# Two heads, or four batches, per chunk over the partitions, A before B, and one buffer ring, in a cached-attention decode kernel

## The chip, the cores and the metric

The kernel runs on one core of one Trainium2 chip. The metric is the device time of one execution in microseconds (us). The kernel before takes 1435.16 us, the median of three runs (1434.9 to 1435.97).

Engines are named as in the profile: PE (matmuls; PEld is its weight load), DVE (vector), ACT (scalar), POOL (GpSimd) and SP, which issues nearly all DMAs (295 of 297 in the DMA view of the kernel before).

## The reference

Two independent attention decode steps, each with one query token per batch and four batches. A has 32 query heads that share 8 key/value heads and looks at the last 2048 keys only. B has 32 heads with their own keys and values and looks at all 8192. The results are concatenated.

```python
def _A_ref(x, k_cache, v_cache, wq, wo):          # 4 batches, D = 512, Dh = 128
    W = min(4096, max(256, Sk // 4))              # 2048
    q = (x @ wq).reshape(B, Sq, Hq, Dh).transpose(0, 2, 1, 3)
    k = jnp.repeat(k_cache[:, :, Sk - W:, :], rep, axis=1)     # rep = 4
    v = jnp.repeat(v_cache[:, :, Sk - W:, :], rep, axis=1)
    p = softmax(einsum("bhqd,bhkd->bhqk", q, k) * Dh ** -0.5)
    o = einsum("bhqk,bhkd->bhqd", p, v)
    return o.transpose(0, 2, 1, 3).reshape(B, Sq, Hq * Dh) @ wo
# _B_ref: the same without window and repeat, 32 heads of 8192 keys
```

Everything is bf16. B's caches are 537 MB, A's windows 33.5 MB, the weights 17 MB. All of it is read once, so the kernel is a long stream of loads with some matmuls behind it.

## The kernel before

One chunk is 2 MB of K and 2 MB of V: one head of one batch (B), or one KV head of all four batches (A). For each 128 keys PE transposes K (T), multiplies it with the query (S), and later multiplies V with the probabilities (PV). B's 128 chunks come first, A's 8 last. K has a ring of 4 buffers and V one of 5.

A chunk always fills all 128 partitions with one DMA. In B a partition gets 64 consecutive keys, one contiguous run of 16 KB in HBM. In A it gets 16 consecutive keys of each batch, four runs of 4 KB:

```python
def kv_src(T, ch):
    if ch["ab"] == 1:
        return T[ch["b"], ch["h"]].rearrange("(p j) d -> p (j d)", p=P)
    return T[:, ch["g"], SkA - W:, :].rearrange("b (p j) d -> p b (j d)", p=P)

def dma_k(c):                                     # dma_v likewise, ring of NVB = 5
    ...
    waits = [("T", (c - NKB + 1) * NG - 1)] if c >= NKB else []
    sch.add_dma("sp", lambda e: e.dma_start(dst, src), ..., waits=waits, key=("k", c))
```

The scores of a chunk are 64 columns in B and 256 in A (64 tiles of 4 queries, each tile of one batch). The loads of the last three V come after all K:

```python
loads.insert(min(2 * c + 1, NC - 1 + c) if c < NC - 3 else len(loads), ("v", c))
```

## Time and profile before

| | value | where it is read |
|---|---|---|
| span | 1432.8 us | page |
| PE, DVE, ACT busy | 84%, 41%, 29% | page, part 1 |
| DMA share on the plateau | 0.99 to 1.01 at 415 to 426 GB/s | windows |
| chain that ended last | 79% DMA | page, part 4 |

The page's rows of the 40 equal slices, and the chain that ended last:

```profile
DMA  9999999999999999999999999999999999998995
GB/s 401 422 425 424 424 423 425 424 427 420 425 424 425 424 423 424 426 425 422 422 426 424 408 416 423 425 424 393 423 426 422 414 411 426 422 419 345 367 398 223
...
DMA 79%; PE 19%; DVE 1%; issue 0%; SPq 0%; ACT 0%; DVEq 0%
```

The DMA engines are busy for 80% or more of every slice but the last. The windows view of the same kernel (columns: the stretch in us, its length, busy us and number of instructions of each engine, granted PE clock, share of the DMA engines, GB/s):

```profile
40.00:80.00 40.00, 33.84 (x803) 32.41 (x800) 17.20 (x35) 12.76 (x22) 0.00 (x0) 1.00 1.01 426
800.00:1000.00 200.00, 168.96 (x3842) 159.39 (x3839) 82.39 (x173) 61.00 (x93) 0.00 (x0) 0.98 0.99 415
1280.00:1320.00 40.00, 33.85 (x784) 31.87 (x781) 16.74 (x36) 12.29 (x19) 0.00 (x0) 1.00 0.87 359
1360.00:1400.00 40.00, 32.04 (x659) 28.46 (x659) 18.40 (x51) 9.99 (x12) 0.00 (x0) 0.96 1.03 397
1420.00:1433.00 13.00, 9.54 (x172) 6.22 (x169) 1.21 (x4) 0.00 (x0) 0.00 (x0) 0.85 0.02 7
```

The first lines are B, the third is the turn to A, the fourth is A with its 4 KB runs, the last is the tail without loads.

The trace also has a record of every DMA packet. In the kernel before, the median packet takes 46 ns for 1 KB, 159 ns for 4 KB, 613 ns for 16 KB and 1213 ns for 32 KB (only the two query weights have runs of that length). So time per byte falls a little as runs grow: 46 ns a KB at 1 KB, 38.3 at 16 KB, 37.9 at 32 KB.

### The profile page before, as it was taken

To read this page: it belongs to the slowest core of one execution; us is meant where nothing else is said; L and a number is where in the kernel's file an instruction comes from. 1 tells how busy PE (TensorE), PEld (TensorE's weight loads), DVE (VectorE), ACT (ScalarE), POOL (GpSimd) and SP (SyncE) were. 2 spreads that over 40 slices of the span, in tenths; PEclk is the share of its full clock that TensorE was granted. 3 is DMA by queue.
4 is the path that set the end of the run, shared out by engine and by line. 5 is a ranking of instruction groups with operands and counts; after the bars stand their busy time and mean duration, and the time that the engine had idled before them with its cause. 6 is when DMAs were issued, how large, how long until landed. Compare 5 with 4: busy or idle time off the path is not lost.

```text
span 1432.8 us, 56273 instructions
## 1 busy us (share of the span) xinstructions
PE 1203.7 (84%) x26928; PEld 1133.7 (79%) x26928; DVE 590.2 (41%) x1267; ACT 421.8 (29%) x627; POOL 2.7 (0%) x11
## 2 busy tenths in 40 slices
PE   4888888888888888888898878888988898988787
PEld 4888887877778887888787878788878788887776
DVE  1434444444443443434344434444444343444444
ACT  0323322323222322323232323232322332333221
POOL 0000000000000000000000000000000000000000
PEclk8999999999999999999999999999999999999999
DMA  9999999999999999999999999999999999998995
GB/s 401 422 425 424 424 423 425 424 427 420 425 424 425 424 423 424 426 425 422 422 426 424 408 416 423 425 424 393 423 426 422 414 411 426 422 419 345 367 398 223
DMA packets 54356, 590.83 MB, mean 412 GB/s; under 512 B 4704, under 2 KB 12912, under 8 KB 21104
## 3 DMA queue, kind: packets, MB, share of 16 engines
q1 hardware_dynamic: 54112, 587.23, 97.9%
q8 instruction: 211, 3.46, 1.0%
q14 instruction: 17, 0.14, 0.0%
q10 hardware_dynamic: 16, 0.01, 0.0%
HBM read 587.21 MB, written 0.01 MB: 410 GB/s over the span
## 4 chain that ended last, share of the span: by engine, by line
DMA 79%; PE 19%; DVE 1%; issue 0%; SPq 0%; ACT 0%; DVEq 0%
DMA kn<-in_B_k_cache_dram 66%; PE tr L273 9%; DMA kn<-in_A_k_cache_dram 7%; DMA vn<-in_B_v_cache_dram 5%; PE po L385 4%; PE sc L302 4%; DMA vn<-in_A_wq_dram 2%; PE ms L334 1%; PE ms L320 0%; DVE kt L280 0%; PE fin L415 0%; PE ms L255 0%; PE ms L391 0%; DVE rm L314 0%; DVE tmp L353 0%
## 5 line engine op out<-in xcount | busy, mean ns | idle before, releaser
L273 PE MATMUL tr<-identb,kn 128*128 128x128 bf16 x8704 | 689.5, 224 | 186.4 <-DMA kn<-in_B_k_cache_dram 165.3
L280 DVE COPY kt<-tr 128x1024 bf16<-128x1024 bf16 x726 | 501.9, 691 | 700.9 <-PE tr L273 696.9
L273 PEld LDWEIGHTS tr<-identb,kn 128*128 128x128 bf16 x8704 | 520.6, 100 | 204.6 <-DMA kn<-in_B_k_cache_dram 180.0
L278 ACT ACTIVATE kt<-tr 128x1024 bf16<-128x1024 bf16 x362 | 370.4, 1023 | 856.7 <-PE tr L273 850.9
L385 PE MATMUL po<-pb,vn 128*128 128x64 bf16 x8704 | 450.6, 195 | 10.4 <-issue 9.3
L302 PE MATMUL sc<-qs,kt 128*128 128x64 bf16 x8704 | 453.3, 195 | 4.5 <-issue 3.6
L302 PEld LDWEIGHTS sc<-qs,kt 128*128 128x128 bf16 x8704 | 377.8, 100 | 10.3 <-issue 4.8
L385 PEld LDWEIGHTS po<-pb,vn 128*128 128x128 bf16 x8704 | 344.1, 99 | 23.9 <-issue 22.7
L342 ACT ACTIVATE pb<-sc,negb 128x64 bf16<-128x64 f32 x128 | 39.9, 312 | 122.5 <-DVE negb L336 122.5
L334 PE MATMUL ms<-gm,nsc 1*128 1x1 f32 x256 | 48.5, 256 | 0.5 <-issue 0.4
L334 PEld LDWEIGHTS ms<-gm,nsc 1*128 1x128 f32 x256 | 37.5, 182 | 14.1 <-issue 0.5
L322 DVE TENSOR_REDUCE gm<-ms 1x1 f32<-1x128 f32 (+1 forms) x136 | 37.0, 272 | 20.6 <-PE ms L320 20.6
L314 DVE TENSOR_REDUCE rm<-sc 128x1 f32<-128x64 f32 (+1 forms) x136 | 31.3, 230 | 29.1 <-PE sc L302 29.1
L320 PE MATMUL ms<-identf,rm 128*1 128x128 f32 (+1 forms) x136 | 38.4, 282 | 1.6 <-DVE rm L314 1.6
L336 DVE COPY negb<-ms 128x1 f32<-128x1 f32 (+1 forms) x136 | 20.8, 153 | 30.0 <-PE ms L334 30.0
L342 ACT ACTIVATION_READ_ACCUMULATOR pb<-sc,negb 128x1 f32 x128 | 25.1, 196 | 0.0
L415 PE MATMUL fin<-wor,oT 128*4 128x512 bf16 x64 | 21.1, 393 | 2.7 <-DVE oT L398 2.7
L320 PEld LDWEIGHTS ms<-identf,rm 128*1 128x1 f32 (+1 forms) x136 | 11.6, 85 | 13.5 <-DVE rm L314 13.4
L255 PE MATMUL ms<-xT,vn 128*128 128x4 bf16 x256 | 7.1, 166 | 10.4 <-DMA vn<-in_A_wq_dram 6.0
L398 DVE TENSOR_TENSOR oT<-po,rinv 128x4 bf16<-128x4 f32 (+1 forms) x40 | 6.3, 158 | 21.9 <-PE po L385 21.9
L255 PEld LDWEIGHTS ms<-xT,vn 128*128 128x128 bf16 x256 | 7.0, 104 | 10.6 <-DMA vn<-in_A_wq_dram 6.1
L391 PE MATMUL ms<-rs,onesf 128*128 128x4 f32 (+1 forms) x80 | 13.8, 244 | 1.1 <-DVE rs L360 1.1
(26 smaller groups left out, 51.7 us busy)
## 6 DMA issues: line engine op xcount, KB each, us to landing
kn<-in_B_k_cache_dram SPq DMA_DIRECT2D x128, 2048.0 KB, 32.4
vn<-in_B_v_cache_dram SPq DMA_DIRECT2D x128, 2048.0 KB, 36.9
kn<-in_A_k_cache_dram SPq DMA_DIRECT2D x8, 2048.0 KB, 20.7
vn<-in_A_v_cache_dram SPq DMA_DIRECT2D x7, 2048.0 KB, 21.9
vn<-in_B_wq_dram SPq DMA_DIRECT2D x1, 4096.0 KB, 12.2
vn<-in_A_wq_dram SPq DMA_DIRECT2D x1, 4096.0 KB, 27.3
wor<-in_B_wo_dram SPq DMA_DIRECT2D x8, 512.0 KB, 37.9
wor<-in_A_wo_dram SPq DMA_DIRECT2D x8, 512.0 KB, 18.3
```

Source lines behind the costliest of these rows:

```text
L273: sch.add("pe", lambda e, o=o, i_=i_: e.transpose(o, i_, identb[:, :]), waits=waits, key=("T", s) if t == TG - 1 else None)
L278: sch.add("act", lambda e: e.activation(dst, src, ACTF.Copy), waits=waits, key=("ev", s))
L280: sch.add("dve", lambda e: e.tensor_copy(dst, src), waits=waits, key=("ev", s))
L302: sch.add("pe", lambda e, o=o, l=l, q=q: e.matmul(o, l, q, start=True, stop=True), waits=waits, key=("S", s) if t == TG - 1 else None)
L314: sch.add("dve", lambda e: e.tensor_reduce(out=dst, in_=src, axis=AX.X, op=ALU.max), waits=[("S", (c + 1) * NG - 1)], key=("rowmax", c))
L320: sch.add("pe", lambda e: e.transpose(ms[0:n, col:col + P], rm[:, m, 0:n], identf[:, :]), waits=[("rowmax", c), "c_identf"] + ms_read, key ...
L322: sch.add("dve", lambda e: e.tensor_reduce(out=gm[0:n, m, :], in_=ms[0:n, col:col + P], axis=AX.X, op=ALU.max), waits=[("trm", c)], key=(" ...
L334: sch.add("pe", lambda e: e.matmul(ms[:, col:col + n], nsc[0:n, :], rhs, start=True, stop=True), waits=[("dg", c) if n > 1 else ("gmax", c ...
L336: sch.add("dve", lambda e: e.tensor_copy(negb[:, m, 0:n], ms[:, col:col + n]), waits=[("bc", c)], key=("negb", c))
L342: sch.add("act", lambda e: e.activation(pbv, sc[:, c % 2, 0:NT], ACTF.Exp, bias=negb[:, m, 0:1], scale=scale, accum_out=ri), waits=[("negb ...
L385: sch.add("pe", lambda e, o=o, l=l, r=r, jj=jj: e.matmul(o, l, r, start=(jj == 0), stop=(jj == J - 1)), waits=waits, key=("pv", c) if j == ...
L415: sch.add("pe", lambda e, o=o, l=l, r=r, st=st, sp_=sp_: e.matmul(o, l, r, start=st, stop=sp_), waits=[("oT", c), ("wo", ch["wo_i"])] if i ...
```

## The change

The intent is longer HBM runs. A B chunk becomes two heads of one batch: head 0 on partitions 0 to 63, head 1 on 64 to 127, 128 keys per partition, runs of 32 KB, 4 MB per load. An A chunk becomes four batches on 32 partitions each, 64 keys per partition, runs of 16 KB. As the partitions of a tile now belong to different heads or batches, the probability matrix has a column for each (2 in B, 16 in A) and zeros in the other blocks, so that one matmul still serves the tile. A goes first, so that its small chunks are not at the end. K and V share one ring of ten 2 MB halves, and the last V comes in four pieces.

```diff
+        chunks.append(dict(ab=0, U=NB, C=REP, g=g, wo=g, NT=NB * W // P, norm=g, last=True, n0=0))
+            chunks.append(dict(ab=1, U=2, C=1, hp=hp, b=b, wo=Hkv + hp // 2, NT=2 * SkB // P, ...))
-        kn = sb("kn", [P, NKB, NT * P], BF16)
-        vn = sb("vn", [P, NVB, NT * P], BF16)
+        kv = sb("kv", [P, NH, 8192], BF16)                       # NH = 10
...
+            if ch["ab"] == 0:
+                PP = P // NB
+                for b in range(NB):
+                    src = T[b, ch["g"], SkA - W:, :].rearrange("(pp j) d -> pp (j d)", pp=PP)
+                    sch.add_dma("sp", lambda e, b=b, src=src: e.dma_start(kv[b * PP:(b + 1) * PP, at, :], src),
+                                "d_h%d" % at, waits=waits, key=(kind, c) if b == NB - 1 else None)
                 return
+            src = T[ch["b"], 2 * ch["hp"]:2 * ch["hp"] + 2].rearrange("u (pp j) d -> (u pp) (j d)", pp=P // 2)
...
+            for u, pp in blocks(c):        # A: each block of partitions keeps its own 4 of 16 columns
+                src = sc[pp, half, :].rearrange("p (j x) -> p j x", x=16)[:, :, u * REP:(u + 1) * REP]
+                sch.add("dve", lambda e, src=src, dst=dst: e.tensor_copy(dst, src), ...)
...
-            loads.insert(min(2 * c + 1, NC - 1 + c) if c < NC - 3 else len(loads), ("v", c))
+            loads.insert(2 * c + 1 if c < NC - 3 else len(loads), ("v", c))
```

Cut: the row maximum, exponential and sum on blocks of partitions, PV waits by ring slot, and the schedule.

## The prediction

> **What bounds the kernel now.** The DMA engines. In the windows view their busy share is 0.99 to 1.01 from 40 to 1280 us, at 415 to 426 GB/s; PE is busy 84% of the span, DVE 41%, ACT 29%. The chain of waits is 79% DMA, nearly all K loads. So bytes, time per packet and the ends of the program matter. The DMA packet records give that time: median 46 ns for 1 KB, 159 ns for 4 KB (A's K and V), 613 ns for 16 KB (B's), 1213 ns for 32 KB (the two wq loads): about 13 ns plus 600 ns for each 16 KB.
>
> A's 8192 packets of 4 KB run at 371 to 397 GB/s (windows 1320 to 1400). At the turn from B to A (1280 to 1320) the rate falls to 359 GB/s, about 6 us lost. After the last loads (about 1417 us) PE still multiplies late V chunks; the span ends at 1432.8, about 16 us in which the DMA does almost nothing.
>
> **What the change does.** Bytes and PE work (8704 transposes, score and PV matmuls each) stay. Costs on DMA:
> - B: 16384 packets of 32 KB: 16384 x 1213 / 16 = 1242 us for 1255; gain 13 us.
> - A: 4 KB becomes 16 KB; gain 4 us by the medians, and about 6 us of the dip at the turn.
> - Tail: the last V comes in pieces, the last of 16 tiles; the PV of the two chunks before is done by then. After the last landing: 16 matmuls, scaling, two output matmuls, a copy, the store: about 6 us for 16; gain 10 us.
> - Ring of ten halves: I estimate over 14 us of queued loads at the tightest moment, so no new waits. Statistics on half or quarter partitions add DVE and ACT operations of 0.2 to 0.4 us; both have room.
>
> The sum is -33 us: about 1401 us, if A's loads run at full rate.
>
> **The doubt.** A's chunk is now loaded by four DMAs of 32 partitions. [...] No DMA of before has this shape, so its trace can't say. [...] I give this 55%.
>
> **Prediction.** 1440 us, eight in ten between 1396 and 1480. Faster by over 2%: 0.38; within 2%: 0.35; slower by over 2%: 0.27. All of it is critical, as DMA is the bound throughout.
>
> **What would show it.** B's packets: 1213 ns, about 428 GB/s on the plateau. [...] Tail: under 7 us from the last V landing to the end. Chain of waits: still K loads, no ring wait that empties the DMA.
>
> **What would make it wrong.** [...] PE stalls in A's longer statistics chain that delay slot release; 4 MB granularity emptying the queue; a slow engine among 16 that sets each landing.

Without the doubt the sum came to -33 us, about 1401 us. The doubt, that A's new loads run slower, put 40 to 78 us on it (1440 to 1480 us) at 55%. These 40 to 78 us rested on no trace. The 0.2 to 0.4 us of a statistics operation are what the trace of the kernel before has (means of 0.15 to 0.42 us). For the 6 us of the tail the same trace has 1.99 us for 64 PV matmuls, 1.04 us for four output matmuls and 0.68 us for the last copy.

## The result, and the profile after

The change takes 1507.2 us (1506.58 to 1508.09, 4 runs) against 1435.03 us: ratio 1.0503, 95% interval [1.0485, 1.0521]. It is 5% slower, outside the stated range.

The page of the kernel after, its slices and chain:

```profile
DMA  9999999999999999999999999999999999999995
GB/s 313 211 215 218 217 339 427 429 429 426 426 428 429 427 424 429 427 427 424 417 421 413 426 426 412 428 412 424 425 418 418 423 425 422 419 419 425 423 424 223
...
DMA 56%; PE 33%; issue 4%; DVE 4%; SPq 2%; another core or an unknown queue 0%; ACT 0%; DVEq 0%
```

And its windows view:

```profile
80.00:120.00 40.00, 22.10 (x346) 19.88 (x344) 17.04 (x40) 5.75 (x8) 0.00 (x0) 0.76 1.01 214
240.00:280.00 40.00, 34.02 (x831) 32.40 (x826) 17.65 (x33) 13.85 (x20) 0.00 (x0) 1.00 1.01 429
800.00:1000.00 200.00, 166.03 (x3825) 158.16 (x3823) 83.20 (x160) 63.06 (x93) 0.00 (x0) 0.96 1.00 420
1480.00:1490.00 10.00, 9.31 (x236) 8.87 (x233) 5.57 (x10) 3.37 (x4) 0.00 (x0) 1.00 0.49 205
1490.00:1500.00 10.00, 9.16 (x290) 8.89 (x291) 0.75 (x4) 0.91 (x4) 0.00 (x0) 1.00 0.28 113
```

The loss has a place. While A is loaded, up to about 210 us, the DMA engines count as fully busy (1.01) and move 214 GB/s. They are not waiting: each packet takes twice as long. In the packet records of 80 to 120 us the median 16 KB packet takes about 1235 ns, where the kernel before needs 613 ns for that size, and the 1 KB packets of the output weights in between take about 90 ns, not 46. A DMA share of 1 does not say that the loads run at full rate; the GB/s beside it does. PE, at 55% in this stretch, is not the limit.

Priced from these records: 2048 packets of 16 KB times (1230 - 613) ns over 16 engines is 79 us, and 4096 packets of 1 KB times 45 ns over 16 is 12 us.

B then runs at 425 to 429 GB/s, against 424 before, but only up to about 600 us; from 600 to 800 us it is 424, later 420 to 422. And in the tail the DMA engines don't finish together: the share is 0.49 at 1480 to 1490 us and 0.28 at 1490 to 1500. The landings shown further down fit this: eight of 16 come near 1480 us, the other eight near 1496.

### The profile page after: what moved, and what is told of

Its sections match the earlier page's. It is cut to its first block, busy times and chain, and to the rows that moved or that the text cites. A ratio compares the mean times of both kernels' runs of the same rounds, so it can differ in the third digit from the quotient of the medians.

```text
span 1504.7 us, 55575 instructions
## 1 busy us (share of the span) xinstructions
PE 1184.0 (79%) x26704; PEld 1124.8 (75%) x26704; DVE 622.7 (41%) x1211; ACT 443.5 (29%) x651; POOL 4.5 (0%) x12
## 3 DMA queue, kind: packets, MB, share of 16 engines
q8 instruction: 208, 3.41, 0.9%
## 4 chain that ended last, share of the span: by engine, by line
DMA 56%; PE 33%; issue 4%; DVE 4%; SPq 2%; another core or an unknown queue 0%; ACT 0%; DVEq 0%
DMA kv<-in_B_k_cache_dram 48%; PE tr L310 15%; PE po L437 8%; PE sc L340 8%; DMA kv<-in_A_k_cache_dram 8%; SPq L225 2%; DVE kt L317 2%; PE ms L392 1%; DVE rm L369 1%; PE ms L376 1%; PE fin L473 0%; DVE rsa L419 0%; ACT pba L417 0%; DVE sA L354 0%
## 5 line engine op out<-in xcount | busy, mean ns | idle before, releaser
L310 PE MATMUL tr<-identb,kv 128*128 128x128 bf16 x8704 | 708.5, 227 | 172.0 <-DMA kv<-in_B_k_cache_dram 83.2
L310 PEld LDWEIGHTS tr<-identb,kv 128*128 128x128 bf16 x8704 | 535.3, 102 | 185.1 <-DMA kv<-in_B_k_cache_dram 89.1
L437 PE MATMUL po<-pbb,kv 128*128 128x64 bf16 x8192 | 419.1, 194 | 50.9 <-issue 50.7
L437 PEld LDWEIGHTS po<-pbb,kv 128*128 128x128 bf16 x8192 | 319.6, 99 | 63.6 <-issue 63.0
L405 ACT ACTIVATE pbb<-sc,negb 64x128 bf16<-64x128 f32 x128 | 51.5, 402 | 81.8 <-DVE negb L394 80.5
L369 DVE TENSOR_REDUCE rm<-sc 64x1 f32<-64x128 f32 x128 | 36.5, 286 | 17.6 <-PE sc L340 16.7
L437 PE MATMUL po<-pba,kv 128*128 128x64 bf16 x512 | 32.8, 219 | 1.5 <-issue 1.1
L392 PE MATMUL ms<-identf,gx 1*128 1x1 f32 (+1 forms) x144 | 28.4, 264 | 2.4 <-DVE gx L384 1.8
L437 PEld LDWEIGHTS po<-pba,kv 128*128 128x128 bf16 x512 | 25.7, 115 | 5.2 <-issue 4.7
L405 ACT ACTIVATION_READ_ACCUMULATOR pbb<-sc,negb 64x1 f32 x128 | 23.7, 185 | 0.0
```

The source lines that it names most:

```text
L310: sch.add("pe", lambda e, o=o, i_=i_: e.transpose(o, i_, identb[:, :]), waits=waits, key=("T", s) if t == TG - 1 else None)
L369: sch.add("dve", lambda e, src=src, pp=pp: e.tensor_reduce(out=rm[pp, m, 0:1], in_=src, axis=AX.X, op=ALU.max), waits=[("S", ch["s_last"]) ...
L392: sch.add("pe", lambda e: e.matmul(ms[:, col:col + C], gx[0:C, m, :], identf[0:C, 0:C], start=True, stop=True), waits=[("gx", c)] + ms_rea ...
L405: sch.add("act", lambda e, src=src, pp=pp, ri=ri, u=u: e.activation(pbv[pp, :, u], src, ACTF.Exp, bias=negb[pp, m, 0:1], scale=scale, accu ...
L437: sch.add("pe", lambda e, o=o, l=l, r=r, j=j: e.matmul(o, l, r, start=(j == 0), stop=(j == ch["NT"] - 1)), waits=waits, key=("pv", c) if j ...
```

## The experiments

The main theory: that each of A's DMAs covers only 32 neighbouring partitions is what halves its rate, and this alone costs the time. Rivals: the small size and larger number of A's DMAs; going first; A's longer statistics chain; the one ring. Runs marked wrong load other data; their amount of work is that of the change unless said otherwise.

### One DMA over 128 partitions (wrong)

```diff
-                for b in range(NB):
-                    src = T[b, ch["g"], SkA - W:, :].rearrange("(pp j) d -> pp (j d)", pp=PP)
-                    ... e.dma_start(kv[b * PP:(b + 1) * PP, at, :], src) ...
+                src = T[ch["g"] % NB, ch["g"], :, :].rearrange("(pp j) d -> pp (j d)", pp=P)
+                ... e.dma_start(kv[:, at, :], src) ...
```

> A's K and V come in one DMA of 128 partitions with 16 KB runs, from a contiguous 2 MB (other rows of the cache, so the result is wrong on purpose); everything else stays. Theory [...]: the first 210 us go from 213 to about 415 GB/s, A's 16 KB packets from a median of 1225 to 613 ns, the 1 KB wo packets between them from about 90 to 46 ns, and the time falls by 79 + 11 = 90 us, to about 1417 us. Rival (A first, its longer statistics chain, or 16 KB runs themselves are slow): packets stay near 1.2 us and the time within 15 us of 1507.

Measured: 1424.77 us, ratio to before 0.9938 [0.9921, 0.9955]. A's rate is back, and so is the packet time (median 611 to 615 ns). Windows view of this run:

```profile
80.00:120.00 40.00, 30.26 (x555) 27.14 (x556) 26.09 (x58) 12.13 (x19) 0.00 (x0) 0.87 1.02 416
120.00:160.00 40.00, 31.76 (x593) 27.86 (x591) 22.71 (x47) 11.99 (x17) 0.00 (x0) 0.87 0.90 366
600.00:1000.00 400.00, 335.24 (x7809) 320.98 (x7807) 170.79 (x326) 127.78 (x187) 0.00 (x0) 0.96 1.00 423
```

The change got 82 us back (1507.2 - 1424.8), 8 less than expected. The second line shows where about 5 of these are: at the turn to B the rate falls to 366 GB/s for 40 us. There SP is held back by PE. In the waits of SP, the output-weight loads of A wait 63.7 us in all for PE's last matmuls of an A chunk, and every later load waits behind them; in the dip itself a load of B waits 16.8 us for PE (from 119.2 to 136.1 us in the trace), and just then the queue runs empty. Whether A's longer statistics or PE's other work is what holds PE was not separated: the dip is gone with the old statistics (423 GB/s at 120 to 160 us, the run with the old A below) and also with the new ones but less PE work (426, the thinned run below). The change hid this behind its slow loads.

### Two DMAs of 64 partitions (wrong)

```diff
+                for i in range(2):
+                    src = T[b, ch["g"], SkA // 2:, :].rearrange("(pp j) d -> pp (j d)", pp=P // 2)   # b by turns
+                    ... e.dma_start(kv[i * 64:(i + 1) * 64, at, :], src) ...
```

> The same bytes, in two DMAs of 64 partitions and 1 MB each (wrong result on purpose). Theory [...] nothing is won: about 213 GB/s and 1.2 us a packet, about 1505 us. Rival (many small DMAs cost the time): half as many DMAs win about half of the 72 us, about 1470 us.

Measured: 1507.06 us, ratio 1.0504 [1.0483, 1.0525]; 215 GB/s at 80 to 120 us. Half as many DMAs of twice the size win nothing, and 64 neighbouring partitions are no better than 32 (215 GB/s against 214):

```profile
80.00:120.00 40.00, 22.59 (x353) 20.25 (x354) 16.23 (x40) 6.27 (x9) 0.00 (x0) 0.74 1.01 215
```

### The same four DMAs on every fourth partition (wrong)

```diff
-                    ... e.dma_start(kv[b * PP:(b + 1) * PP, at, :], src) ...
+                    ... e.dma_start(kv[b:P:NB, at, :], src) ...
```

> The same four DMAs of 512 KB from the same HBM addresses with the same 16 KB runs, but each lands on every fourth partition instead of 32 neighbouring ones (wrong result on purpose). Theory [...]: the set of partitions alone sets the rate. [...] about 415 GB/s and 613 ns, 1417 us[...]. Rival (size or number of the DMAs, or the HBM addresses): unchanged, 213 GB/s and 1507 us.

Measured: 1426.67 us, ratio 0.9944 [0.9924, 0.9964], median packet 611 ns. Windows view:

```profile
80.00:120.00 40.00, 28.06 (x535) 24.99 (x532) 27.37 (x62) 12.88 (x20) 0.00 (x0) 0.91 0.98 398
```

This is the sharpest of the three. HBM addresses, run length, size and number of the DMAs are those of the change. Only the set of partitions differs, and nearly the whole loss is gone (398 GB/s against 214). So the set of partitions is the cause; the size and number of the DMAs are not. Why the set of partitions matters, no trace here shows.

### Both halves queued at once, from two queues

A's batches 0 and 1 are issued from SP, 2 and 3 from GpSimd, with their own semaphores. The result is right.

```diff
-                    sch.add_dma("sp", ...)
+                    sch.add_dma("sp" if b < 2 else "pool", ...)
```

> The change with A's four DMAs of 32 partitions split over two queues: batches 0 and 1 (partitions 0 to 63) from SP, batches 2 and 3 (partitions 64 to 127) from GpSimd[...]. The result is right. [...] nothing is won: 16 KB packets near 1.2 us, about 1507 us. [...] up to twice the rate in the first 210 us, down to 1430 us. If the size of the DMAs were the cause, nothing would change either; full_width, half_width and strided speak against that.

Measured: 1509.2 us, ratio 1.0522 [1.0503, 1.0542]. It moves more than the change at 40 to 80 us (238 GB/s against 211) but less before (281 against 307 up to 40 us), then 220. The texts had two outcomes, nothing won or up to twice the rate. In its time this run agrees with the first, but it is a weaker test than planned. The packet records show 16 KB packets of both queues in flight together for only about 40% of 10 to 190 us; for the rest at most one queue had any. Windows view, with both queues at work (first line) and with GpSimd's alone:

```profile
50.00:62.00 12.00, 7.10 (x168) 6.75 (x168) 2.36 (x6) 1.02 (x1) 4.82 (x10) 0.51 1.01 264
66.00:90.00 24.00, 3.87 (x56) 3.51 (x56) 4.93 (x8) 1.72 (x3) 0.97 (x2) 0.62 1.01 219
```

So even with both halves at work the rate was 264 GB/s, far from the 416 of one DMA over 128 partitions, and the median packet took about 1.0 us. The packets in flight swing there from 1 of one queue and 15 of the other to 15 and 1 and back, every 4 us: nearly all packets in flight change queues together. Why they do was not looked into.

### A as in the kernel before, everything else as in the change

A's load, scores and statistics are taken back to the old form (one DMA over 128 partitions with 4 KB runs); A still goes first, the ring is the new one, and B keeps its two heads. The result is right.

```diff
-                for b in range(NB): ... e.dma_start(kv[b * PP:(b + 1) * PP, at, :], src) ...
+                src = T[:, ch["g"], SkA - W:, :].rearrange("b (p j) d -> p b (j d)", p=P)
+                dst = kv[:, at, :].rearrange("p (b x) -> p b x", b=NB)
+                ... e.dma_start(dst, src) ...
-                    bank, o0, col = j // HT, 16 * (j % HT), 16 * ch["g"]
+                    bank, o0, col = c % 2, REP * j, 16 * ch["g"] + REP * (j // JA)
     (and the row maximum, shift, exponential, sum and PV of A as before)
```

> The change with one part undone: A's chunk is loaded and computed as in the kernel before (one DMA over 128 partitions, 4 KB runs, 16 columns of statistics, one activation), still first and in the one ring; B keeps two heads a chunk. The result is right. Theory [...]: the whole loss goes, and more: full_width needed 1424.8 us; 4 KB packets cost 4 us more by their medians, the shorter chain of A gives back some 5 us of the dip at the turn from A to B. 1418 to 1428 us, faster than before by about 1%. Rival (going first or the one ring is what costs): over 1450 us.

Measured: 1422.34 us, ratio 0.9920 [0.9906, 0.9933] over five rounds. It beats both kernels, by 0.8% and 5.6%. Going first and the single ring are not what costs. A's packing also wins nothing once each load of A covers all 128 partitions: with 4 KB runs A runs at 401 to 408 GB/s here, with 16 KB runs at 416, but the turn to B is smooth:

```profile
80.00:120.00 40.00, 29.91 (x610) 26.31 (x606) 17.92 (x50) 9.33 (x11) 0.00 (x0) 0.96 1.03 408
120.00:160.00 40.00, 33.02 (x690) 30.39 (x690) 18.67 (x40) 12.36 (x16) 0.00 (x0) 0.92 1.02 423
```

### What B's longer runs are worth (wrong)

The 128-partition variant with B's two heads as two DMAs of 16 KB runs:

```diff
-            sch.add_dma("sp", lambda e: e.dma_start(dst, src), ...)
+            for u in range(2):
+                su = T[ch["b"], 2 * ch["hp"] + u].rearrange("(p j) d -> p (j d)", p=P)
+                ... e.dma_start(kv[:, at + u, :], su) ...
```

> The full-width variant with one more step: B's two heads come as two DMAs over 128 partitions with 16 KB runs instead of one with 32 KB (wrong result on purpose). It prices the longer runs alone. Theory (13 ns a packet, and 613 against 1213 ns): 32768 packets instead of 16384, the time rises by 10 to 13 us over 1424.8. Rival (run length beyond 16 KB is worth nothing; the gain over before comes from elsewhere): within 3 us of 1424.8.

Measured: 1432.46 us, ratio 0.9989 [0.9975, 1.0003]. Against the 128-partition variant (ratio 0.9938) that is 0.0051 of 1434 us, about 7 us. So the longer runs are worth about 7 us, with the two intervals taken together 4 to 11, which is probably less than the 10 to 13 expected. The packet records don't explain the shortfall. The means of these two runs themselves, 621 ns for 16 KB and 1232 ns for 32 KB, promise (2 x 621 - 1232) x 16384 / 16 = 10 us; those of the kernels before and after, 619.4 and 1235.7 ns, promise only 3. Why they differ, and which part of the 7 us is the packets', stays open: the lead of half the engines (next section) differs between these two runs as well.

### The missing gain: which engines finish last

Without a loss on A's loads I had predicted 1401 us; the variants above without it give 1422 to 1427. The trace has 16 landing events for each load; I take each to be the part of one of the 16 DMA engines, but the trace does not name the engines. For one load near 750 us, and for the last V, sorted, in us:

```
before        729.3  729.3  729.3  729.4  729.8  729.8  731.7  734.2 |  749.1  749.6  750.6  750.9  751.0  751.0  751.0  751.2
after         731.3  731.3  731.5  731.6  732.2  732.2  732.5  735.6 |  747.4  747.6  749.0  749.1  749.2  749.7  750.3  750.5
after, last V 1480.0 1480.2 1480.2 1480.2 1480.3 1480.3 1480.4 1480.6 | 1494.4 1494.7 1495.9 1496.0 1496.1 1496.6 1497.1 1497.3
```

Eight landings come 15 to 20 us ahead of the other eight. In both kernels the lead (mean of the first eight against the last eight) grows by 2.8 us per 100 us at first, then it stops growing, near 23 us before and 16 us after. From about then on the rate falls: 424 to 415 GB/s before, 427 to 420 after. My reading, not shown by a trace, is that the fast eight have used up the ring and wait, and all go at the pace of the slow eight. At the end, half of the engines are idle for about 15 us: in the packet records of the kernel after, 16 packets are in flight at 1470 to 1479 us and only 8 at 1482 to 1493. The growth is not the same in all variants (2.1 us per 100 us in the 128-partition one, and with B's 16 KB runs the lead stops at 5 us); that is not explained here.

One suspect is the instruction stream. The page of the kernel after has a DMA queue of the kind "instruction" (queue 8: 208 packets, 3.41 MB, so 16 KB each), and each packet took a median of 1.06 us; I call these packets fetches. The page counts them with those of the loads, as 0.9% of the time of the 16 DMA engines. Three runs looked at this.

First, the 128-partition variant with 5 of 8 PE matmuls left out (wrong; the same loads, fewer instructions, less PE work):

```diff
+                if t not in (0, 4, TG - 1):
+                    continue
                 sch.add("pe", ... e.transpose / e.matmul ...)
```

> The full-width variant with 5 of 8 transposes, score and value matmuls left out (wrong result on purpose): about 20 thousand PE instructions instead of 53 thousand, the same loads. Theory (the instruction fetches, 3.4 MB in 208 packets of about 1.07 us[...]): the landings of the two halves of a load drift apart by under 1.2 us per 100 us instead of about 3, and the slow eight finish 10 to 20 us earlier: about 1405 us, of which up to 5 us may be the dip at the turn. Rival [...]: the drift stays near 3 us per 100 us, and the time within 7 us of 1424.8.

Measured: 1391.18 us, ratio 0.9701 [0.9683, 0.9719], 34 us less than the 128-partition variant; more than expected. About 4 of the 34 us are a shorter end (4.4 us after the last landing, not 8.1), and about 6 the dip at the turn that is gone; both go with PE's smaller work. The instruction packets fall from 208 to 81, the lead grows by 1.0 us per 100 us between 230 and 500 us, and the plateau holds 429 to 430 GB/s to the end:

```profile
600.00:1000.00 400.00, 220.65 (x2974) 190.83 (x2975) 165.56 (x325) 127.61 (x187) 0.00 (x0) 0.64 1.00 429
```

This run took away two things, instructions and PE work. The control, each left-out matmul replaced by one of a single row and column, failed:

```diff
                 if t not in (0, 4, TG - 1):
+                    sch.add("pe", lambda e, ...: e.matmul(o[0:1, 0:1], l[0:1, 0:1], q[0:1, 0:1], ...), waits=waits)
                     continue
```

> few_instr with each left-out matmul replaced by one of a single row and column (wrong result on purpose): the instruction count is that of the change again (about 53 thousand on PE, 208 instruction packets), the PE work stays small. It separates the two things few_instr took away. Theory (fetched instructions take DMA time[...]): the landings drift apart by 2 to 3 us per 100 us again instead of 1, the plateau falls from 429 to about 424 GB/s, and the time goes back up by 15 to 30 us, to 1406 to 1421 us. Rival (less PE work frees the slots earlier[...]): 1391 us again, 429 GB/s, drift 1.

Measured: 2402.38 us, ratio 1.6752. PE was busy 99% of the span, at a granted clock of 0.5, so the run says nothing of DMA. Such a matmul took 159 ns in the page:

```profile
L342 PE MATMUL sc<-qs,kt 1*1 1x1 bf16 x5440 | 429.5, 159 | 0.0
L344 PE MATMUL sc<-qs,kt 128*128 128x64 bf16 x3264 | 787.7, 241 | 0.0
```

The second control put the instructions elsewhere: the thinned kernel with 22000 one-element memsets on the idle GpSimd, for which nothing waits.

```diff
+        for i in range(22000):
+            sch.add("pool", lambda e, i=i: e.memset(junk[:, i % 11000:i % 11000 + 1], 0), ...)
```

> few_instr with 22 thousand one-element memsets added on the idle GpSimd engine, which nothing waits for (wrong result on purpose). tiny_mm failed as a control because PE became the bound; this adds fetched instructions without PE work. 22000 [...] (3.41 MB for 55.6 thousand instructions in the change) are 1.35 MB, about 82 more packets of 1.07 us. Theory (fetched instructions take DMA time from the loads): 82 x 1.07 / 16 = 5.5 us more if they spread over all engines, up to 11 us if they fall on eight: 1397 to 1402 us, and the lead of one half of the engines grows by more than the 1.0 us per 100 us of few_instr. Rival (only PE's smaller work made few_instr fast): 1391 us, unchanged within 1.5 us.

Measured: 1490.5 us, ratio 1.0390 [1.0373, 1.0408], 99 us over the thinned kernel: the direction of the theory, but 9 to 18 times its 5.5 to 11 us. Page (queue 14 carries GpSimd's instructions here) and windows view:

```profile
q8 instruction: 81, 1.33, 0.4%
q14 instruction: 188, 1.54, 0.3%
...
600.00:1000.00 400.00, 206.17 (x2712) 178.92 (x2709) 156.75 (x301) 117.28 (x174) 265.41 (x7937) 0.61 0.93 385
1000.00:1200.00 200.00, 111.41 (x1516) 96.15 (x1517) 83.83 (x165) 65.34 (x95) 0.00 (x0) 0.66 1.00 426
```

While GpSimd works, up to about 950 us, the loads run at 385 GB/s; as soon as it stops, at 426. A load near 750 us landed like this:

```
729.4  729.5  729.6  729.6  729.6  729.7  729.8  729.8  729.9  729.9  729.9  730.0  730.0  730.2  731.2  754.8
```

One of the 16 landings is 24 us behind all others, so presumably one engine is late, and the whole stream waits for it. So it is shown that instructions elsewhere on the core can slow the loads (385 GB/s against 429) without more PE work; that one late engine then sets the time is my reading of this load. That the fetches do it is likely but not isolated, since the memsets also write SBUF and no run had the one without the other. Two things speak for the fetches: only one of 16 landings is late, and GpSimd itself stops 171 times (204.8 us in all, in the waits view), as often as there are packets added on queue 14 (188, where the kernel after has 17). Not settled: the 171 added packets, of 8 KB each, at 309 ns are 53 us of one engine's time, and the loss is 99 us; and how much of the 34 us of the thinned kernel is due to fetches and how much to PE's smaller work.

Second question: does the depth of the ring matter? The 128-partition variant with eight halves:

```diff
-NH = 10
+NH = 8
```

> The full-width variant with a ring of eight halves instead of ten. Theory (the slower eight engines set the time; a deeper queue only lets the others run ahead): the lead of the fast eight stops at a smaller value (under 12 us instead of 17), the time stays within 6 us of 1424.8. Rival (the ring's depth or its waits cost time in the change): the time rises by over 15 us, and the DMA share falls below 0.97 on the plateau.

Measured: 1434.93 us, ratio 1.0006 [0.9988, 1.0024]: 10 us more, 4 beyond the band. The lead of the fast eight stops near 5 to 7 us, as expected, and the plateau stays at 420 GB/s (600 to 1000 us), close to the 423 of ten halves. The loss is mostly at the turn from A to B, where the smaller ring has less to bridge with:

```profile
120.00:160.00 40.00, 32.23 (x604) 28.38 (x600) 23.52 (x49) 12.44 (x17) 0.00 (x0) 0.87 0.68 272
```

From 366 to 272 GB/s over 40 us is 40 x 94 / 424 = 9 us.

### The tail

In the kernel before, the last load has landed at 1422.2 us, and the span ends 10.6 us later. In the kernel after, these are 1497.3 us and 7.4 us. Of the 10 us that I had counted on, 3 came. The chain that ended last, last pieces (start in us, length in us, what), before:

```profile
1419.12 2.57 PE po L385 x48
1421.95 1.87 PE fin L415 x4
1423.82 1.99 PE po L385 x64
1426.06 1.03 PE fin L415 x4
1427.08 1.99 PE po L385 x64
1429.39 1.04 PE fin L415 x4
```

And after:

```profile
1487.71 0.56 PE tr L310 x7
...
1491.41 1.92 PE po L437 x62
1493.34 0.31 issue
1493.65 6.79 PE po L437 x226
1500.64 0.73 PE po L437 x24
1501.69 0.61 PE fin L473 x2
```

After, the end is one chain on PE without any wait for a load. The last two K chunks come back to back (V is put off), PE transposes them until 1488 us, and only then does the remaining PV. I had written that this PV would be done by the time the last V lands. Two runs on the right-result variant with the old A test it.

```diff
-LASTV = (64, 32, 16, 16)
+LASTV = (128,)
```

> a_old_layout with the last V chunk in one DMA instead of four pieces. It prices the pieces at the end. Theory: the last landing stays where it was, but all 128 value matmuls (about 4 us) come after it instead of 16: the time rises by 3 to 4 us over a_old_layout, whose ratio to before was 0.9920, so to about 0.9945. If another chain already ends last there, the ratio stays within 0.001.

Measured: 1423.44 us, ratio 0.9925 [0.9912, 0.9939] against 0.9920. The pieces are worth nothing that can be measured, as PE is not there yet when they land (with the four pieces it works 9.3 us past the last landing).

```diff
-            loads.insert(2 * c + 1 if c < NC - 3 else len(loads), ("v", c))
+            loads.insert(2 * c + 1 if c < NC - 1 else len(loads), ("v", c))
     (and the extra delay of the third-last PV is dropped)
```

> a_old_layout with the loads of the last three chunks in the usual order (K and V in turn), instead of all K before the last three V. The result is right. In a_old_layout the last 45 us are one unbroken chain on PE (transposes of the last two K chunks, which come back to back, then 313 value matmuls), not a wait for the last V. Theory: with V between the K loads PE finishes two value chunks earlier, its backlog after the last K is 4 to 8 us smaller, and the end is then set by the last V landing: 2 to 4 us faster than a_old_layout's 0.9920 of before, so about 0.990. Rival (the tail is not PE's): unchanged, or 3 us slower because the last K lands later.

Measured: 1424.87 us, ratio 0.9936 [0.9922, 0.9949], not faster. The last load lands at 1412.6 us as before (1412.4), but the last K lands later, and PE still works 11.5 us after the last landing, where it was 9.3. My expectation fell and the rival's stood: the usual order is no better than that of the change (the two intervals overlap), and this reordering did not take PE's backlog away.

## Why the prediction was wrong

- **A's loads on 32 partitions (the doubt).** The doubt was named and held: the set of partitions halved the rate. Its odds and its size were off. I gave it 55%; it was there in full. I put it at +40 to +78 us, because I thought that some of the loss would be won back, which rested on no trace. This step failed. Nothing was won back: A ran at 211 to 220 GB/s from 40 to 160 us, with packets of 1.2 us. I also left out that the 1 KB packets of the output weights, between A's loads, double too, 12 us by the packet records. Removing the cause gives 82 us (the 128-partition variant).
- **The rest of the sum.** I had -33 us without the doubt, and the runs show -8 to -12. B's longer runs were put at -13 and are worth about 7 (the 16 KB run); why less stays open. A's longer runs and the turn were put at -10 and are worth nothing that shows: the turn has its own cost in the new form, and the old form of A is as fast or 2 us faster, which is within the noise. The dip at the old turn, which I had counted as 6 us lost, went with the lead of the fast engines falling from 23 to 8 us in the landings; this was only read, not tested. The tail was put at -10 and gave about 3: the step that failed is that the PV of the two chunks before would be done.
- **The ring.** "No new waits" held on the plateau (DMA share 1.00) and in the change itself, but not for a fast A: there the turn starves (366 GB/s at 120 to 160 us in the 128-partition variant).
- **What made the range fail.** The range ended at 1480, my highest estimate of the doubt (78 us) on top of all gains. The full cost, 82 us, with the real gain of 10 us, gives 1507. So of the 27 us beyond the range's end 23 are gains that did not come (33 summed, 10 had) and 4 are cost of A's loads above the highest estimate. The middle, 1440, was low for another reason as well: it gave no more than 55% to a cost that came in full.

## What to carry to other kernels

Look at which partitions a DMA covers before you look at its run length: four DMAs on 32 neighbouring partitions halved the rate here (214 GB/s at 80 to 120 us), and the same four on every fourth partition did not (398). A DMA share of 1 is no proof of full rate (it stood at 1.01 beside these 214 GB/s); read the GB/s and the time of one packet beside it. When costing the end of a load stream, ask which of the 16 landings come last (eight came 15 us after the others here) and what PE still has to do then; a mean or median over the 16 hides the first.
